# Channel attention and a gated convolution on one core: the first batch's rows dealt anew, weight conversion through PSUM, and the first softmax in another order

## The chip, the cores and the metric

One Trainium2 chip, of which the kernel uses one core. The metric is the device time of one execution in microseconds, as the median of several runs.

## The reference

Four batches of 6336 positions by 256 channels. An attention over channels is made of q and k, applied to v, and its result goes through a gated convolution over positions.

```python
qn = q / (np.linalg.norm(q, axis=1, keepdims=True) + 1e-06)
kn = k / (np.linalg.norm(k, axis=1, keepdims=True) + 1e-06)
s = kn.transpose(0, 2, 1) @ qn / tau          # 256 x 256 per batch, summed over 6336 positions
a = np.exp(s - s.max(-1, keepdims=True))
a /= a.sum(-1, keepdims=True) + 1e-09
x = v @ a                                      # 6336 x 256 per batch
# gated convolution, 5 taps over the positions, weights conv_w per channel
gate = sigmoid(sum_k conv_w[k] * x shifted by 4 - k positions)
out = (gate * (x @ w_val)) @ w_out
```

All data are fp32, but the three weights of the convolution stage, w_val, conv_w and w_out, arrive as 64-bit floats.

## The kernel before, in words

**Two streams of work.** The scores of a batch need all of its q and k before the softmax can be taken; the outputs of a batch need its softmax. So the kernel runs the scores of a later batch beside the outputs of an earlier one. Only the first batch has nothing beside it: its scores, its softmax and the first chunks of its outputs form a prologue of some 85 us.

**Scores by groups.** The 6336 positions of a batch are 49 rows of 128 positions (row j holds positions j, 49 + j and so on, one per partition) and a rest of 64. They are loaded in 17 groups: group 0 has one row and the rest, groups 1 to 16 three rows each. `score_group(b, g)` (L166) works on one group. The tile `raw` (six buffers) holds q and k of the group. A row can go to TensorE in two ways, chosen by `nw` (L171 to L174): the first `nw` rows of a group go unsplit, as fp32 matmuls of k by q; the other rows are split. For a split row ACT makes a rounded copy `hi` (L192), POOL the difference to it (L193), and TensorE does three products of the parts for each half of the channels (L226). One cast and one difference cover all split rows of a group. In a page of the profile, an unsplit row is four matmul records and a split row six.

**The norms.** ACT squares the group (L209, or L205 for the first row that a sum takes, which is written straight into it) into `sq`, two buffers. The squares are added to one of two sums: rows j < `nv` by VectorE to `acc_ps` in PSUM, the others by POOL to `acc` in SBUF (both L214). Before, batch 0 has `nw, nv = (3, 2)` for groups 0 to 10 and `(2, 3)` from group `SIDE` = 11 on. In batch 1 the first `LEAD` groups are unsplit; every other group is split whole, with `nv` = 2.

**The weights.** `load_weights(part)` (L105) loads the 64-bit words on SP's queue: part 0 is w_val, tau and conv_w, part 1 w_out. `prepare_weights(part)` (L124) is a generator that turns them into fp32 on VectorE in integer and float steps (L132 to L154), each step followed by a yield; its intermediate `f` lies in SBUF, in the tile that takes the result. For w_out a rounded part `wo_hi` (ACT, L149) and a rest `wo_lo` are made. The loads stand in the loop over the first batch's groups at n = 6, and from n = 9 on two steps of each part follow each group.

**The softmax.** `softmax(b)` (L236) is a generator, moved on one stage by each `tick()` (L466): sum the two norm sums and copy the scores out of PSUM (L240, L242); column sums with TensorE (L245, L247); square root, and for batch 0 a dummy exponential that loads ACT's table (L252, L254); reciprocals, scaling and the minimum on VectorE (L256 to L265); exponentials (L268); normalisation (L270 to L275); split into `w` (L278, L279); transposes of the result (L285); their copy (L289); product with w_val (L294); its split (L298, L299). With the first split done the gate's products can run, with the last the values'.

**Outputs by chunks.** v is handled in 13 chunks of 508 positions a batch. `transpose_v` (L326) turns a chunk and splits it into `v_hi` and `v_lo`; `conv` (L352) makes x for the taps (matmuls at L345 into `x_ps`) and applies the taps on ACT (L359) and VectorE (L361); `sigmoid`, `value` (`val_ps`, L374), `split_g` and `finish` (L404, L414) follow.

**What sets the order.** The calls in L476 to L563 are the program order. From it a planner builds the queue of each engine ahead of time, with its own estimate of when instructions become ready; earlier calls go first, and what is called under `tc.high_priority()` (every tick) goes ahead of other work. `behind(engines)` (L433) puts what is called in it, on each named engine, behind the last instruction that was marked in `marks` for that engine. On the chip each engine takes its queue in order. In the prologue, `run_group` (L453) issues the matmuls of a group, and `split_group` (L445) everything before them and the load of the group `PREFETCH` = 4 ahead. The prologue does `LEAD` groups of batch 1 between the stages of the first softmax. In the loop over the 52 chunks, `due` (L531) spreads the groups that are left evenly over the first 36 chunks.

## Time and profile before

| what | value |
|---|---|
| median of 3 runs | 657.26 us (657.15 to 657.44) |
| the profiled execution, its own time | 658.18 us |
| its span in the profile | 656.3 us |
| mean granted TensorE clock | 0.996 |
| busy: PE, VectorE, ACT, POOL | 97%, 80%, 71%, 55% |
| scores of batch 0, last matmul (L226) starts | 54.03 us |
| first matmul of the outputs (L345) | 70.69 us |

PE is TensorE, PEld its weight loads, DVE VectorE, ACT ScalarE, POOL GpSimd. A line of the timeline gives start and length in us, the engine, the line of the kernel, the operation, what it writes and reads, and in square brackets how long the engine had been idle before and what ended this. A line of the groups gives count, busy time in us and mean duration in ns. Matmuls are pipelined and their ends are modelled, so that a matmul's length is more than the distance to the next one, and the distance is what counts. The span begins with the first instruction; the execution's time has about 2 us around it.

### The profile page before, as it was taken

What the parts mean: (1) busy time and instruction counts of PE and PEld (TensorE: products, weight loads), DVE (VectorE), ACT (ScalarE), POOL (GpSimd) and SP (SyncE); (2) the same over time, 40 slices, a digit from 0 to 9 for tenths busy, and PEclk for the clock granted to TensorE, in tenths of its full rate; (3) what the DMA queues carried; (4) which work ended last, traced back from release to release, by engine and by line L of the source; (5) the groups of instructions that cost most, each with busy time, mean ns of one, the idle gap of its engine ahead of it and who ended that gap; (6) DMA issues with size and microseconds to landing.
All of it is one profiled execution on the core that took longest, in us unless ns stands there. A gap on an engine that the chain in (4) does not pass through costs nothing.

```text
span 656.3 us, 10656 instructions
## 1 busy us (share of the span) xinstructions
PE 637.8 (97%) x4008; PEld 571.1 (87%) x4008; DVE 523.0 (80%) x832; ACT 466.1 (71%) x607; POOL 360.8 (55%) x173
## 2 busy tenths in 40 slices
PE   7989999999999999999998999999999999999996
PEld 5868799989979999999997998998999798888886
DVE  3898689787878688778788688778778888888894
ACT  4565978867888768668698687767777756655564
POOL 2442796965837769659565497766763222312220
PEclk9999999999999999999999999999999999999999
DMA  8999874555635565545564365563222343443213
GB/s 268 322 328 337 267 225 152 161 166 165 179 103 176 188 195 176 173 132 170 175 184 121 109 217 158 189 185 104 65 78 71 118 126 95 121 129 104 65 50 100
DMA packets 107875, 105.75 MB, mean 161 GB/s; under 512 B 5744, under 2 KB 107312, under 8 KB 107824
## 3 DMA queue, kind: packets, MB, share of 16 engines
q1 hardware_dynamic: 81520, 79.24, 39.0%
q10 hardware_dynamic: 26304, 25.84, 13.9%
q8 instruction: 31, 0.51, 0.3%
q14 instruction: 20, 0.16, 0.1%
HBM read 79.11 MB, written 25.95 MB: 160 GB/s over the span
## 4 chain that ended last, share of the span: by engine, by line
PE 85%; ACT 5%; DVE 4%; POOL 2%; DMA 2%; issue 1%; SPq 1%; ACTq 0%; POOLq 0%
PE o_ps L404 20%; PE x_ps L345 20%; PE val_ps L345 19%; PE s_ps L226 18%; PE t_ps L335 6%; POOL hi L193 1%; ACT sq L209 1%; PE o_ps L294 1%; DMA raw<-in_k_dram 1%; DVE acc_ps L214 1%; ACT hi L192 1%; DVE gate L361 1%; DMA v_raw<-in_v_dram 1%; DVE gate L374 1%; ACT gate L367 0%
## 5 line engine op out<-in xcount | busy, mean ns | idle before, releaser
L361 DVE SCALAR_TENSOR_TENSOR gate<-x_ps,wa,gate 128x508 f32<-128x508 f32 (+1 forms) x416 | 275.4, 716 | 15.7 <-ACT gate L359 14.6
L193 POOL TENSOR_TENSOR hi<-raw,hi 128x1536 fp32r<-128x1536 f32 (+2 forms) x54 | 167.8, 3110 | 94.5 <-ACT hi L192 94.5
L388 POOL TENSOR_TENSOR g_lo<-gate,g_hi 128x1016 fp32r<-128x1016 f32 (+1 forms) x50 | 116.6, 2332 | 145.2 <-ACT g_hi L387 130.6
L214 DVE TENSOR_TENSOR acc_ps<-acc_ps,sq 128x512 f32<-128x512 f32 (+1 forms) x134 | 93.4, 697 | 74.8 <-ACT sq L209 71.6
L345 PE MATMUL x_ps<-v_hi,w 128*128 128x512 f32 (+1 forms) x416 | 139.1, 394 | 0.0
L345 PE MATMUL val_ps<-v_hi,w 128*128 128x508 f32 (+1 forms) x416 | 133.9, 383 | 0.8 <-ACT o_sb L414 0.7
L226 PE MATMUL s_ps<-hi 128*128 128x256 f32 (+1 forms) x852 | 121.1, 287 | 7.4 <-ACT hi L192 4.0
L226 PEld LDWEIGHTS s_ps<-hi 128*128 128x128 f32 (+1 forms) x852 | 110.7, 190 | 13.9 <-ACT hi L192 5.5
L404 PE MATMUL o_ps<-wo_hi,g_hi 128*128 128x256 f32 x400 | 113.2, 283 | 1.7 <-ACT g_hi L383 1.5
L414 ACT COPY o_sb<-o_ps 128x512 f32<-128x512 f32 x99 | 58.2, 589 | 79.1 <-PE o_ps L404 77.9
L404 PE MATMUL o_ps<-wo_lo,g_hi 128*128 128x256 f32 x400 | 112.1, 280 | 0.0
L404 PE MATMUL o_ps<-wo_hi,g_lo 128*128 128x256 f32 x400 | 111.7, 280 | 0.0
L209 ACT ACTIVATE sq<-raw 128x1536 f32<-128x1536 f32 (+3 forms) x69 | 96.0, 1393 | 16.5 <-DVE acc_ps L214 7.9
L214 POOL TENSOR_TENSOR acc<-acc,sq 128x512 f32<-128x512 f32 x58 | 76.4, 1318 | 39.7 <-ACT sq L209 39.3
L345 PEld LDWEIGHTS x_ps<-v_hi,w 128*128 128x128 f32 x416 | 78.2, 190 | 14.3 <-DVE gate L361 0.2
L345 PEld LDWEIGHTS val_ps<-v_hi,w 128*128 128x128 f32 x416 | 77.1, 188 | 14.5 <-ACT o_sb L414 0.9
L359 ACT ACTIVATE gate<-x_ps,wa 128x508 f32<-128x508 f32 (+1 forms) x104 | 68.2, 671 | 20.5 <-PE x_ps L345 20.2
L336 ACT CAST v_hi<-t_ps 128x512 fp32r<-128x512 f32 (+1 forms) x104 | 55.8, 569 | 36.2 <-PE t_ps L335 36.2
L345 PE MATMUL x_ps<-v_lo,w 128*128 128x512 f32 (+1 forms) x208 | 80.2, 386 | 0.0
L345 PE MATMUL val_ps<-v_lo,w 128*128 128x508 f32 (+1 forms) x208 | 79.2, 381 | 0.0
L374 DVE TENSOR_TENSOR gate<-val_ps,gate 128x508 f32<-128x508 f32 (+1 forms) x104 | 64.3, 657 | 18.3 <-ACT gate L367 14.0
L404 PEld LDWEIGHTS o_ps<-wo_hi,g_hi 128*128 128x128 f32 x400 | 75.2, 188 | 3.1 <-ACT g_hi L383 1.7
(84 smaller groups left out, 799.3 us busy)
## 6 DMA issues: line engine op xcount, KB each, us to landing
raw<-in_q_dram SPq DMA_DIRECT2D x64, 384.0 KB
raw<-in_k_dram SPq DMA_DIRECT2D x64, 384.0 KB
v_raw<-in_v_dram SPq DMA_DIRECT2D x44, 512.0 KB
out_dram<-o_sb ACTq DMA_DIRECT2D x48, 384.0 KB
out_dram<-o_sb ACTq DMA_DIRECT2D x48, 124.0 KB
v_raw<-in_v_dram SPq DMA_DIRECT2D x4, 384.0 KB
raw<-in_q_dram SPq DMA_DIRECT2D x4, 128.0 KB
raw<-in_k_dram SPq DMA_DIRECT2D x4, 128.0 KB
```

The source lines that it names most:

```text
L193: nc.gpsimd.tensor_tensor(hi[r, js, :, 1, :], raw[r, js, :, :], hi[r, js, :, 0, :].bitcast(F32), ALU.subtract)
L209: nc.scalar.activation(sq[0:np_, ja:jb], raw[0:np_, ja:jb], AF.Square)
L214: eng.tensor_tensor(st[key][0:np_], st[key][0:np_], sq[0:np_, j], ALU.add)
L226: nc.tensor.matmul(st["s"][:, h, :], lhs, rhs, start=False, stop=stop and h == NH - 1 and n_ == len(ops) - 1)
L336: nc.scalar.copy(th[:, h, 0:w], tp[:, 0:w])
L345: nc.tensor.matmul(ps, wt[:, which, ws, ch, hs], vs[:, ch, lo:hi_], start=n_ == 0, stop=n_ == 3 * NH - 1)
L359: nc.scalar.activation(gate[:, h, 0:w], x_ps[:, 0:w], AF.Copy, scale=cw[:, h, 0:1])
L361: nc.vector.scalar_tensor_tensor(gate[:, h, 0:w], x_ps[:, tap:tap + w], cw[:, h, tap:tap + 1], gate[:, h, 0:w], ALU.mult, ALU.add)
L374: nc.vector.tensor_tensor(gate[:, h, 0:w], val_ps[:, 0:w], gate[:, h, 0:w], ALU.mult)
L388: nc.gpsimd.tensor_tensor(gl[:, :, 0:w], gate[:, :, 0:w], gh[:, :, 0:w].bitcast(F32), ALU.subtract)
L404: nc.tensor.matmul(o_ps[:, u * C:(u + 1) * C], gs[:, h, off:off + P], ws[:, h, :], start=n_ == 0, stop=n_ == 3 * NH - 1)
L414: marks["ACT"] = nc.scalar.copy(o_sb[:, j:j + len(pair), :], o_ps[:, 0:len(pair) * C].rearrange("p (j c) -> p j c", c=C))
```

## The change

- Rows of batch 0: `nw, nv` are (3, 2) for group 0, (1, 3) for groups 1 to 5 (`EARLY` = 6), then (2, 2) for even and (3, 1) for odd groups.
- `LEAD` is 4 instead of 5: four groups of batch 1 in the prologue.
- The weights come in three parts, all loaded at n = 1, into buffers of other tiles ("gate", "o_sb") and one of their own. The intermediate of the conversion lies in PSUM. The parts are converted one after the other, three or four steps after each group from n = 7 on, on VectorE behind the last add of the norms. `wo_hi` is made by a copy on ACT behind the first softmax.
- The first softmax: the transposes of the first chunk come right behind the last scores of batch 0, the column sums behind these; the groups of batch 1 stand elsewhere between the ticks. More instructions are marked.

```diff
--- before.py
+++ after.py
@@ -17,10 +17,10 @@
 
 P = 128
 GROUP = 3
-LEAD = 5
+LEAD = 4
 PREFETCH = 4
 VLEAD = 2
-SIDE = 11
+EARLY = 6
 HALO = 4
 ROWS = 508
 
@@ -93,42 +93,47 @@
 
 
     WORDS = 2 if w_val.dtype == I64 else 1
-    NA = NH * C + NH * K
-    wa = const.tile([P, NA], F32, name="wa")
-    wb = const.tile([P, NH * C], F32, name="wb")
-    wv_sb = wa[:, 0:NH * C].rearrange("p (h e) -> p h e", h=NH)
-    cw = wa[:, NH * C:].rearrange("p (h k) -> p h k", h=NH)
+    NW = NH * C
+    wa = const.tile([P, NW + NH * K], F32, name="wa")
+    wb = const.tile([P, NW], F32, name="wb")
+    wv_sb = wa[:, 0:NW].rearrange("p (h e) -> p h e", h=NH)
+    cw = wa[:, NW:].rearrange("p (h k) -> p h k", h=NH)
     wo_hi = const.tile([P, NH, C], F32R, name="wo_hi")
     wo_lo = const.tile([P, NH, C], F32R, name="wo_lo")
+    parts_w = {"val": wa[:, 0:NW], "conv": wa[:, NW:], "out": wb}
     w_raw = {}
 
-    def load_weights(part):
-        src, w = ((w_val, wa), (w_out, wb))[part]
-        if WORDS == 2:
-            pool, tag = ((split_p, "hi"), (w_p, "o_sb"))[part]
-            raw = pool.tile([P, w.shape[1], WORDS], I32, name="w_raw", tag=tag)
-            src = src.bitcast(I32)
-        else:
-            raw = w.rearrange("p (n o) -> p n o", o=1)
-        w_raw[part] = raw
-        nc.sync.dma_start(out=raw[:, 0:NH * C, :].rearrange("p (h e) o -> p h (e o)", h=NH),
-                          in_=src.rearrange("(h p) e -> p h e", p=P))
-        if part == 0:
-            nc.sync.dma_start(out=tau_sb, in_=tau.broadcast_to([P, 1]))
-            src = conv_w.bitcast(I32) if WORDS == 2 else conv_w
-            for h in range(NH):
-                nc.sync.dma_start(
-                    out=raw[:, NH * C + h * K:NH * C + (h + 1) * K, :],
-                    in_=src[:, h * P * WORDS:(h + 1) * P * WORDS].rearrange("k (p o) -> p k o", o=WORDS))
+    def load_weights():
+        for part, w in parts_w.items():
+            if WORDS == 2:
+                tag = {"val": "gate", "out": "o_sb"}.get(part)
+                raw = (w_p if tag else const).tile([P, w.shape[1], WORDS], I32, name="w_raw", tag=tag or "c_raw")
+            else:
+                raw = w.rearrange("p (n o) -> p n o", o=1)
+            w_raw[part] = raw
+            if part == "conv":
+                src = conv_w.bitcast(I32) if WORDS == 2 else conv_w
+                nc.sync.dma_start(out=tau_sb, in_=tau.broadcast_to([P, 1]))
+                for h in range(NH):
+                    nc.sync.dma_start(out=raw[:, h * K:(h + 1) * K, :],
+                                      in_=src[:, h * P * WORDS:(h + 1) * P * WORDS].rearrange("k (p o) -> p k o", o=WORDS))
+            else:
+                src = {"val": w_val, "out": w_out}[part]
+                src = src.bitcast(I32) if WORDS == 2 else src
+                nc.sync.dma_start(out=raw.rearrange("p (h e) o -> p h (e o)", h=NH),
+                                  in_=src.rearrange("(h p) e -> p h e", p=P))
 
     def prepare_weights(part):
 
 
 
-        w = (wa, wb)[part]
+
+        w = parts_w[part]
+        n = w.shape[1]
         if WORDS == 2:
             lo, up = w_raw[part][:, :, 0], w_raw[part][:, :, 1]
-            f = w.bitcast(I32)
+            fs = ps.tile([P, 512], F32, name="w_ps", tag="bank")[:, 0:n]
+            f = fs.bitcast(I32)
             nc.vector.tensor_scalar(f, up, 0x1FF, 15, ALU.bitwise_and, ALU.logical_shift_left)
             yield
             nc.vector.scalar_tensor_tensor(lo, lo, 17, f, ALU.logical_shift_right, ALU.bitwise_or)
@@ -145,18 +150,15 @@
             yield
             nc.vector.tensor_tensor(up, up, f, ALU.bitwise_or)
             yield
-            if part:
-                nc.scalar.copy(wo_hi.rearrange("p h e -> p (h e)"), up.bitcast(F32))
-            dst = w if part == 0 else wo_lo.rearrange("p h e -> p (h e)")
-            nc.vector.scalar_tensor_tensor(dst, lo, 2.0 ** -35, w, ALU.mult, ALU.mult)
-            if part == 0:
+            dst = wo_lo.rearrange("p h e -> p (h e)") if part == "out" else fs
+            nc.vector.scalar_tensor_tensor(dst, lo, 2.0 ** -35, fs, ALU.mult, ALU.mult)
+            if part != "out":
                 yield
-                nc.vector.tensor_tensor(w, w, up.bitcast(F32), ALU.add)
-        elif part:
-            wof = wb.rearrange("p (h e) -> p h e", h=NH)
-            nc.scalar.copy(wo_hi, wof)
-            nc.vector.tensor_tensor(wo_lo, wof, wo_hi.bitcast(F32), ALU.subtract)
-        if part == 0:
+                nc.vector.tensor_tensor(w, fs, up.bitcast(F32), ALU.add)
+        elif part == "out":
+            nc.vector.tensor_copy(wo_hi, wb.rearrange("p (h e) -> p h e", h=NH))
+            nc.vector.tensor_tensor(wo_lo, wb.rearrange("p (h e) -> p h e", h=NH), wo_hi.bitcast(F32), ALU.subtract)
+        if part == "conv":
             yield
             tc.keep_in_program_order(nc.vector.reciprocal(rtau, tau_sb))
 
@@ -169,7 +171,7 @@
         n = groups[g][1]
         raw = raws.pop((b, g))
         if b == 0:
-            nw, nv = (GROUP, 2) if g < SIDE else (2, 3)
+            nw, nv = (GROUP, 2) if g == 0 else (1, 3) if g < EARLY else (2, 2) if g % 2 == 0 else (GROUP, 1)
         else:
             nw, nv = (GROUP, 1 if g else 2) if b == 1 and g < LEAD else (0, 2)
         parts = [(P, 0, n)]
@@ -211,7 +213,9 @@
             if j in where:
                 continue
             eng, key = (nc.vector, "acc") if j < nv else (nc.gpsimd, "side")
-            eng.tensor_tensor(st[key][0:np_], st[key][0:np_], sq[0:np_, j], ALU.add)
+            add = eng.tensor_tensor(st[key][0:np_], st[key][0:np_], sq[0:np_, j], ALU.add)
+            if key == "acc":
+                marks["DVE"] = add
 
         def mms(np_, j):
             r = slice(0, np_)
@@ -223,8 +227,8 @@
                 else:
                     ops = [(hi[r, j, 1, x, hs], hi[r, j, 0, y, :]) for x, y in ((0, 0), (0, 1), (1, 0))]
                 for n_, (lhs, rhs) in enumerate(ops):
-                    nc.tensor.matmul(st["s"][:, h, :], lhs, rhs, start=False,
-                                     stop=stop and h == NH - 1 and n_ == len(ops) - 1)
+                    marks["PE"] = nc.tensor.matmul(st["s"][:, h, :], lhs, rhs, start=False,
+                                                   stop=stop and h == NH - 1 and n_ == len(ops) - 1)
 
         def clear():
 
@@ -239,7 +243,7 @@
         acc = soft_p.tile([P, 2, C], F32, name="acc_all")
         nc.vector.tensor_tensor(acc, st["acc"], st["side"], ALU.add)
         s = soft_p.tile([P, NH, C], F32, name="s")
-        nc.scalar.copy(s, st["s"])
+        marks["ACT"] = nc.scalar.copy(s, st["s"])
         yield
         n_ps = ps.tile([P, 512], F32, name="o_ps", tag="bank")
         nc.tensor.matmul(n_ps[:, 0:C], ones, acc[:, 0, :], start=True, stop=True)
@@ -262,7 +266,7 @@
         for h in range(NH):
             nc.vector.scalar_tensor_tensor(s[:, h, :], s[:, h, :], nk[:, h:h + 1], r, ALU.mult, ALU.mult)
         m = soft_p.tile([P, NH], F32, name="m")
-        nc.vector.tensor_reduce(m, s, axis=AX.X, op=ALU.min)
+        marks["DVE"] = nc.vector.tensor_reduce(m, s, axis=AX.X, op=ALU.min)
         yield
         for h in range(NH):
             marks["ACT"] = nc.scalar.activation(s[:, h, :], s[:, h, :], AF.Exp, scale=-1.0, bias=m[:, h:h + 1], accum_out=z[:, h:h + 1])
@@ -332,7 +336,7 @@
         tp = ps.tile([P, 512], F32, name="t_ps", tag="bank")
         for j in range(-(-w // P)):
             np_ = min(P, w - j * P)
-            nc.tensor.transpose(tp[:, j * P:j * P + np_], src[0:np_, j, h * P:(h + 1) * P], ident[0:np_, 0:np_])
+            marks["PE"] = nc.tensor.transpose(tp[:, j * P:j * P + np_], src[0:np_, j, h * P:(h + 1) * P], ident[0:np_, 0:np_])
         nc.scalar.copy(th[:, h, 0:w], tp[:, 0:w])
         nc.vector.tensor_tensor(tl[:, h, 0:w], tp[:, 0:w], th[:, h, 0:w].bitcast(F32), ALU.subtract)
 
@@ -474,10 +478,9 @@
 
 
     for n in range(NG):
-        if n == 6:
-            load_weights(0)
-            load_weights(1)
-            prep.extend(prepare_weights(part) for part in range(2))
+        if n == 1:
+            load_weights()
+            prep.extend(prepare_weights(part) for part in parts_w)
         if n == NG - 4:
             load_upto(NG + 1)
             with tc.issue_after(last_load[0].ins):
@@ -487,36 +490,40 @@
                 for nv in range(1, VLEAD + 1):
                     load_v(*step(nv))
         run_group()
-        if n >= 9:
-            for gen in prep:
-                for _ in range(2):
-                    next(gen, 0)
+        if n > EARLY:
+            with behind("DVE"):
+                for _ in range(3 + n % 2):
+                    while prep and next(prep[0], 0) is not None:
+                        prep.pop(0)
     for gen in prep:
         for _ in gen:
             pass
-    prep.clear()
-    run_group()
     tick()
-    tick()
+    with tc.high_priority(), behind("PE", "ACT"):
+        for h in range(NH):
+            transpose_v(*step(0), h)
+    with behind("PE"):
+        tick()
+    with behind("ACT"):
+        run_group()
     tick()
     with behind("PE", "ACT"):
-        run_group()
-        for h in range(NH):
-            transpose_v(*step(0), h)
-    tick()
-    tick()
-    with behind("ACT"):
         run_group()
     tick()
     tick()
     tick()
+    tick()
     with behind("ACT"):
-        for n in range(3, LEAD):
+        for n in range(2, LEAD):
             run_group()
+    tick()
     for h in range(NH):
         conv(*step(0), h)
     while stages:
         tick()
+    if WORDS == 2:
+        with behind("ACT"):
+            nc.scalar.copy(wo_hi.rearrange("p h e -> p (h e)"), w_raw["out"][:, :, 1].bitcast(F32))
     for h in range(NH):
         transpose_v(*step(1), h)
     with behind("ACT"):
```

## The prediction

> **What bounds the kernel now.** I read the page first, for the engines' shares; then the windows of 25 us over the whole span, for the stretches where TensorE is not full; then the timeline of the first 90 us and of the one long gap behind it, and the duration of matmuls by stretch.
>
> ```profile
> span 656.3 us, 10656 instructions
> PE 637.8 (97%) x4008; PEld 571.1 (87%) x4008; DVE 523.0 (80%) x832; ACT 466.1 (71%) x607; POOL 360.8 (55%) x173
> 25.00:50.00 25.00, 22.20 (x111) 19.07 (x111) 24.27 (x35) 15.26 (x15) 12.01 (x9) 1.00 1.08 335
> 75.00:100.00 25.00, 23.69 (x150) 20.54 (x149) 21.53 (x34) 20.66 (x22) 23.31 (x11) 1.00 0.71 220
> 350.00:375.00 25.00, 22.31 (x144) 20.27 (x143) 17.67 (x30) 20.12 (x31) 9.64 (x5) 0.93 0.38 119
> ```
>
> The columns of a window are its length, then busy time (instructions) of PE, PEld, DVE, ACT and POOL, the granted clock, the DMA share and GB/s. TensorE is full in most windows, so the end comes earlier only by what is taken from TensorE's own work, its gaps, or its time at a low clock. In 25 to 50 us VectorE is full and TensorE is not: that is the stage that the change rebuilds.
>
> ```profile
> L226 PE MATMUL s_ps<-raw x6: 634/634/634, 9.7 to 11.9; 128*128 128x256 f32 x6
> L226 PE MATMUL s_ps<-raw x11: 379/379/379, 13.8 to 16.0; 128*128 128x256 f32 x11
> 4.31 20.04 PE L226 MATMUL s_ps<-raw 128*128 128x256 f32 x70 [1.91 <-DMA raw<-in_k_dram]
> 23.75 14.84 PE L226 MATMUL s_ps<-raw 128*128 128x256 f32 x68
> 92.69 2.15 PE s_ps L226 x18
> ```
>
> An unsplit row is 4 instructions. From 23.75 us on they start every 14.84/68 = 0.218 us, 0.87 us a row. A split row is 6 instructions at 2.15/18 = 0.119 us, 0.72 us a row. Until about 13 us the same unsplit instruction lasts 634 ns instead of 379, and six start within 2.2 us, one every 0.43 us: TensorE works at half rate there, although the granted clock reads 1.00. It has no gap from 4.31 to 38.6 us.
>
> ```profile
> 35.78 1.48 ACT L209 ACTIVATE sq<-raw 128x1536 f32<-128x1536 f32 x1 [3.43 <-DVE acc_ps L214]
> 40.15 0.86 PE L226 MATMUL s_ps<-hi 128*128 128x256 f32 x5 [1.44 <-POOL hi L193]
> 44.47 0.86 PE L226 MATMUL s_ps<-hi 128*128 128x256 f32 x5 [0.97 <-POOL hi L193]
> 54.03 1.06 PE L226 MATMUL s_ps<-hi 128*128 128x256 f32 x6
> 56.18 0.69 DVE L240 TENSOR_TENSOR acc_all<-acc_ps,acc 128x512 f32<-128x512 f32 x1
> 58.12 0.70 PE L245 MATMUL o_ps<-acc_all,ones 128*128 128x256 f32 x2
> 59.19 0.37 ACT L252 ACTIVATE o_ps<-o_ps 128x258 f32<-128x258 f32 x1 [1.69 <-PE o_ps L247]
> 69.12 0.62 ACT L278 CAST w<-a 128x512 fp32r<-128x512 f32 x1
> 70.69 0.47 PE L345 MATMUL x_ps<-v_hi,w 128*128 128x512 f32 x1
> ```
>
> VectorE, busy with the weight conversion, holds the squares (3.43 us), these hold the casts, and TensorE's first split rows wait for POOL. With the waits for the casts themselves TensorE loses some 3 us from 38.6 to 44.5 us. The scores of batch 0 end at 54.03 + 6 x 0.119 = 54.8 us; the sum of squares follows at 56.2 us, its column sums on TensorE only at 58.1 us, queued behind the first rows of batch 1; the weights of batch 0 reach TensorE at 70.7 us.
>
> **The change, part by part.** First the rows. Unsplit rows of batch 0 fall from 44 to 34, split rows rise from 6 to 16 (two in each of groups 1 to 5, one in each even group from 6): 10 x 0.15 = 1.5 us less for TensorE. But groups 1 to 5 now pass through ACT and POOL before TensorE can finish them, and the load of the weights moves ahead of group 5's.
>
> ```profile
> 8.03 0.63 ACT L205 ACTIVATE acc<-raw 128x512 f32<-128x512 f32 x1 [2.61 <-DMA raw<-in_k_dram]
> 11.33 1.48 ACT L209 ACTIVATE sq<-raw 128x1536 f32<-128x1536 f32 x1 [1.72 <-DMA raw<-in_k_dram]
> 20.34 1.48 ACT L209 ACTIVATE sq<-raw 128x1536 f32<-128x1536 f32 x1 [0.75 <-DVE acc_ps L214]
> 24.72 1.48 ACT L209 ACTIVATE sq<-raw 128x1536 f32<-128x1536 f32 x1 [2.90 <-DMA raw<-in_k_dram]
> 28.66 1.48 ACT L209 ACTIVATE sq<-raw 128x1536 f32<-128x1536 f32 x1 [2.46 <-DMA raw<-in_k_dram]
> 351.43 1.04 ACT L387 CAST g_hi<-gate 128x1016 fp32r<-128x1016 f32 x1 [0.26 <-DVE gate L374]
> L388 POOL TENSOR_TENSOR g_lo<-gate,g_hi 128x1016 fp32r<-128x1016 f32 (+1 forms) x50 | 116.6, 2332 | 145.2 <-ACT g_hi L387 130.6
> L193 POOL TENSOR_TENSOR hi<-raw,hi 128x512 fp32r<-128x512 f32 x6 | 7.9, 1313 | 6.2 <-ACT hi L192 6.2
> ```
>
> Groups 1, 2, 6, 7 and 8 land at 8.0, 11.3, 20.3, 24.7 and 28.7 us; from 2 to 6 that is 2.25 us a group. Today the weights sit around group 7 and hold it back by 24.7 - 22.6 = 2.1 us and group 8 by 28.7 - 27.0 = 1.7 us, 3.8 us together. The new order issues them right behind group 4, so group 5 lands at 18.1 + 3.8 = 21.9 us. A cast and a split of two rows have no row of their own; the nearest, 1016 wide, take 1.04 and 2.33 us (bounds: twice a 512 split, 2.6 us, and no less than 1.3). Both lie on TensorE's path when a group comes late.
>
> Group 1: its unsplit row ends at 9.7 us, cast 9.1, POOL 11.4; then 12 split instructions at half rate, 2.9 us, 14.3. Group 2: 1.7 us at half rate, 16.0; from here I take full rate, 1.4 us, 17.4. Groups 3 and 4 at 0.87 + 1.43: 19.7 and 22.0. Group 5: cast 23.0, POOL 25.3, TensorE 26.7, after a gap of 2.4 us. Groups 6 to 16: 27 unsplit rows, 23.5 us, and 6 split, 4.3 us: 54.5 us. POOL has two items of 1.28 to 1.31 in each of these groups, 2.6 us against TensorE's 2.53 on average, and starts 1.4 us ahead: it just keeps up. So TensorE's 3 us of waits and 1.5 us of work go, and 4.2 us of later starts in groups 1 to 5 eat them. Gain 0.3 us; bounds -2 (POOL at 2.6 us a pair, later groups waiting on it) and +2.8 (group 5 not held).
>
> VectorE's part:
>
> ```profile
> 24.77 0.45 DVE L136 TENSOR_SCALAR wa<-w_raw 128x522 int32<-128x522 int32 x1
> 30.36 1.76 DVE L146 TENSOR_TENSOR w_raw<-w_raw,wa 128x522 int32<-128x522 int32 x1
> 32.49 1.70 POOL L214 TENSOR_TENSOR acc<-acc,sq 128x512 f32<-128x512 f32 x1 [0.94 <-ACT sq L209]
> L214 DVE TENSOR_TENSOR acc_ps<-acc_ps,sq 128x512 f32<-128x512 f32 x37 | 25.8, 696 | 9.7 <-ACT sq L209 8.5
> ```
>
> Nineteen of the new 29 conversion steps are 512 wide. In SBUF they ran from 0.4 to 1.8 us, and POOL's adds beside them 1.7 instead of 1.3. With the intermediate in PSUM none has a row; the nearest is the add on PSUM, 0.70 us (bounds 0.4 and 1.8). At 0.70 they cost 13.3 us, about today's 15, in groups 7 to 9 and 12 to 14. There VectorE needs up to 3.5 us a group, but has one or two adds instead of two or three and catches up in 10, 11, 15 and 16: its last add ends near 53.7 us, beside POOL's 53.8, and acc_all near 54.5, not 56.9. The Trainium skill (VectorE: DVE Perf Modes, Why PSUM operands drop a tier) says that an operand in PSUM takes the doubled fp32 rate from single-source steps. By it the 0.45 us steps become 0.7 us, about 2 us more over both parts, and by the old rate the sum would be those 2 us smaller; both lie beside TensorE's work here.
>
> The softmax:
>
> ```profile
> 61.85 0.87 PE t_ps L335 x8
> 62.15 0.70 DVE L214 TENSOR_TENSOR acc_ps<-acc_ps,sq 128x512 f32<-128x512 f32 x1
> 63.80 1.28 DVE L337 TENSOR_TENSOR v_lo<-t_ps,v_hi 128x512 fp32r<-128x512 f32 x2
> 66.83 1.47 ACT L209 ACTIVATE sq<-raw 128x1536 f32<-128x1536 f32 x1
> ```
>
> Eight transposes now stand behind the last score, 0.87 us, to 55.4 us, then the column sums, 58.12 to 59.19 today, 1.0 us, to 56.4. (If chunk 0's values landed after 54.5 us, the column sums and the rows of batch 1 would wait behind the transposes; they are issued with the last loads of batch 0.) Then a clear (512 wide, 0.2 us) and four groups instead of five: 8 + 36 instructions at 0.217 us, 9.6 us, to 66.2, and the transposes of the weights, so the first x_ps at 66.5. The chain beside it took 69.74 - 59.19 = 10.5 us, of which an add of 0.7, two v_lo of 0.64 and 0.9 of the squares (66.83 to 68.30, while the reciprocals were done at 67.3) came from outside; these are queued elsewhere now. So the weights are there between 64.0 and 67.0. I take 66.7 for x_ps. Today's 70.7 contains the fifth group, 2.6 us, so the like is 68.1: gain 1.4 us with the 0.3 in it. The fifth group's three rows are split in the loop, 2.15 for 2.6 us: 0.45 us. The final copy to wo_hi moves behind the softmax, about 0.6 us on ACT (as the cast of w at 69.12) before its first reader, hidden by the transposes and values that come before; without that cover it costs 0.6. The 1.3 us of gaps from 75 to 100 us (25.00 less 23.69 in the second window above) I leave as they are.
>
> Sum: 1.85 us off the profiled execution, whose own time is 658.2 us, 1.9 around its span. The median stands 0.9 under it: 657.3 - 1.9 = 655.4 us.
>
> **The rivals.** First, faster because of a gap far behind the change: four groups ahead instead of five shift the later batches. The last group of batch 2 comes one step later, and as the first of a step's two groups, not the second.
>
> ```profile
> 354.89 0.28 PE L404 MATMUL o_ps<-wo_hi,g_lo 128*128 128x256 f32 x1
> 357.86 0.53 PE L226 MATMUL s_ps<-hi 128*128 128x256 f32 x1 [2.69 <-ACT hi L192]
> 356.00:358.00 2.00, 0.14 (x1) 0.14 (x2) 2.00 (x5) 2.00 (x3) 0.06 (x1) 0.99 0.31 103
> 358.00:360.00 2.00, 2.00 (x6) 1.61 (x7) 1.06 (x3) 1.99 (x3) 2.00 (x1) 0.50 0.53 122
> 360.00:362.00 2.00, 2.00 (x8) 1.58 (x7) 0.66 (x1) 1.98 (x2) 2.00 (x2) 0.66 0.10 35
> ```
>
> Here TensorE stands from 355.0 to 357.9 us, 2.9 us, and then runs 2 us at a clock of 0.50 and 2 at 0.66: 1.0 + 0.7 = 1.7 us. If the new order of the groups avoids it, 4.6 us more go: 650.8 us. For it: the other two batches, where the softmax starts with a step's first group, have no gap of this size. Against: ACT's exponentials and table load stand ahead of the casts in any order.
>
> Second, group 5 is not held by the weights (they land beside it, or are issued later): scores end near 52, and 655.4 - 2.5 = 652.9 us.
>
> Third, slower: the splits in groups 1 to 5 keep TensorE at half rate. It left the half rate at 13 us only after 8.6 us without a gap; now it waits from 9.7 to 11.4, and 2.4 us ahead of group 5. At half rate a group costs 1.7 + 2.9 = 4.6 us: group 1 at 14.3, then 18.9, 23.5, 28.1, 32.7 for group 5, against 26.7. That is 6 us lost: 661.4 us; half of it, if the rate rises in group 3, 658.4. It decides from the point where waits in the stretch from 9 to 16 us hold the rate down. Against: after the 2.9 us gap the clock was back within 4 us of dense work. The Trainium skill (TensorE: Matmul & The Clock Gate, HAM oscillation — how this bites in real kernels) warns against gaps over about 3.4 us, after which the array runs at half clock. By this 2.4 us would be safe; the 2.9 us gap above was punished all the same, so the measured row decides.
>
> Fourth, no change: the chain keeps its intrusions (weights at 67.0 or later) and the gaps from 75 to 100 us grow by one: 656.6 us.
>
> **How the numbers follow.** Forecast 0.35, own range 653.9 to 656.9; the gap goes 0.24 (650.8); group 5 free 0.12 (652.9); half rate 0.17 (658.4 to 661.4); no change 0.12. What can be told from no change is 0.2%, 1.3 us. Two thirds of the forecast's own range lies beyond it: faster 0.24 + 0.24 + 0.12 = 0.60; same 0.11 + 0.12 - 0.01 = 0.22; slower 0.18. The range runs from 650.6, the gap gone, to 659.2, the half rate until group 3 with some POOL lag.
>
> **What would show it.** Group 5's first square near 22 us and a TensorE gap of 2 to 3 us before its split rows; matmuls of 379 ns from 16 us on; no wait for POOL between 27 and 54 us; last score at 54.5; column sums near 55.5; first x_ps at 66.7. Wrong if TensorE waits for POOL after group 6, if the unsplit instruction still lasts 634 ns past 17 us, if x_ps waits for the weights' cast, or if TensorE's gap at a later softmax comes, goes or moves by more than 2 us.

## The result and the profile after

The changed kernel takes 660.12 us (median of 4 runs, 659.92 to 661.46) against 657.2 us before: 2.9 us more, where 655.4 us was forecast. The ratio of the runs is given as 1.0056, 95% interval 1.0037 to 1.0074 (the quotient of the two medians is 1.0044), so it is slower by about half a per cent. The profiled execution took 660.24 us, with a span of 658.5 us; the forecast for it was 658.2 - 1.85 = 656.35, so 3.9 us are to be found.

The page of the kernel after, busy time of the engines:

```profile
PE 637.0 (97%) x4034; PEld 571.3 (87%) x4034; DVE 522.3 (79%) x837; ACT 471.1 (72%) x613; POOL 382.8 (58%) x184
```

Its windows (length; busy time of PE, PEld, DVE, ACT, POOL; granted clock, DMA share, GB/s):

```profile
25.00:50.00 25.00, 25.00 (x127) 22.66 (x128) 22.94 (x45) 16.62 (x15) 21.92 (x18) 0.94 1.03 322
24.58:28.00 3.42, 3.09 (x13) 3.00 (x14) 3.14 (x5) 2.70 (x3) 1.86 (x3) 0.50 1.10 349
```

TensorE is busy for 0.8 us less than before, POOL for 22 us more. VectorE no longer fills the stretch from 25 to 50 us; POOL nearly does (21.92 of 25). In this execution a low clock stands at 24.58 us: 3.42 us at 0.50, beginning inside a gap of TensorE. It isn't what made the change slower: the other three executions have a mean granted clock of 0.999 to 1.000, which leaves no room for such a stretch (one alone brings the mean to 0.997), and they took 659.92, 659.99 and 661.46 us. The low clock that the profile before had at 358 to 362 us isn't there any more (from 340 to 395 us the clock is 1.00, in the windows below).

The timeline of the kernel after, from the first groups to the first products:

```profile
21.38 1.04 ACT L194 CAST hi<-raw 128x1024 fp32r<-128x1024 f32 x1 [3.35 <-DMA raw<-in_k_dram]
...
24.91 2.71 PE L230 MATMUL s_ps<-hi 128*128 128x256 f32 x11 [2.04 <-POOL hi L195]
...
30.90 0.69 DVE L143 TENSOR_SCALAR w_ps<-w_ps 128x512 int32<-128x512 int32 x1
...
54.38 1.06 PE L230 MATMUL s_ps<-hi 128*128 128x256 f32 x6
...
55.04 0.69 DVE L244 TENSOR_TENSOR acc_all<-acc_ps,acc 128x512 f32<-128x512 f32 x1 [1.10 <-POOL acc L216]
...
56.15 0.60 PE L249 MATMUL o_ps<-acc_all,ones 128*128 128x256 f32 x2
...
57.01 1.05 ACT L340 CAST v_hi<-t_ps 128x512 fp32r<-128x512 f32 x2
...
57.95 0.37 ACT L256 ACTIVATE o_ps<-o_ps 128x258 f32<-128x258 f32 x1
...
60.91 0.70 DVE L216 TENSOR_TENSOR acc_ps<-acc_ps,sq 128x512 f32<-128x512 f32 x1 [1.34 <-ACT sq L211]
...
61.52 1.76 DVE L262 RECIPROCAL o_ps<-o_ps 128x256 f32<-128x256 f32 x1
...
67.80 0.62 ACT L282 CAST w<-a 128x512 fp32r<-128x512 f32 x1
...
68.47 0.50 PE L349 MATMUL x_ps<-v_hi,w 128*128 128x512 f32 x1 [0.21 <-ACT w L282]
```

Group 5 lands at 21.4 us, and TensorE waits 2.04 us for its split. The last scores start at 54.38 us, 0.35 later than before. The column sums come 2.0 us earlier than before (56.15 against 58.12), but the long reciprocal, at 60.28 before, comes at 61.52: squares and casts of the first chunk now stand ahead of the square root, and an add that waits 1.34 us for its squares stands ahead of the reciprocal. The first products start 2.2 us earlier than before, with one group (2.6 us) less ahead of them. So at the door of the loop (the first products) nothing is won: in like terms it opens 0.4 us later. The rest of the 2.2 us that the span grew is lost behind it.

The loop of the kernel after, in windows around the softmaxes of batches 1 and 2:

```profile
185.00:235.00 50.00, 47.36 (x319) 42.80 (x319) 39.05 (x67) 41.96 (x62) 29.17 (x13) 1.00 0.51 151
340.00:395.00 55.00, 52.43 (x356) 47.67 (x355) 44.02 (x75) 44.95 (x64) 31.08 (x15) 1.00 0.53 156
```

TensorE's waits there from 185 to 235 us (what waited, for what, us in total, times, longest):

```profile
PE s_ps L230 <- POOL hi L195: 1.2, 2, 0.6
PE t_ps L339 <- ACT at L293: 0.9, 1, 0.9
PE val_ps L349 <- ACT o_sb L418: 0.6, 1, 0.6
```

The same two windows of the kernel before:

```profile
185.00:235.00 50.00, 49.21 (x340) 44.98 (x339) 39.25 (x69) 40.29 (x56) 32.88 (x15) 1.00 0.56 167
340.00:395.00 55.00, 52.31 (x349) 47.87 (x348) 42.34 (x75) 43.82 (x61) 31.64 (x15) 0.97 0.51 157
```

At batch 1 TensorE stands 50 - 47.36 = 2.64 us after, 0.79 before. At batch 2 it stands 2.57 us after and 2.69 before, but before this was one gap with a low clock behind it; after it is several short waits. So something new costs near 2 us at batch 1 and stands in the place of the gap at batch 2, though the loop over the chunks is not in the diff.

### The profile page after: what moved, and what is told of

Read it like the earlier page. It is cut to its first block, busy times and chain, and to the rows that moved or that the text cites. A ratio compares the mean times of both kernels' runs of the same rounds, so it can differ in the third digit from the quotient of the medians.

```text
span 658.5 us, 10744 instructions
## 1 busy us (share of the span) xinstructions
PE 637.0 (97%) x4034; PEld 571.3 (87%) x4034; DVE 522.3 (79%) x837; ACT 471.1 (72%) x613; POOL 382.8 (58%) x184
## 4 chain that ended last, share of the span: by engine, by line
PE 81%; ACT 9%; DMA 3%; issue 2%; POOL 2%; DVE 1%; SPq 1%; ACTq 0%; POOLq 0%
PE o_ps L408 20%; PE s_ps L230 19%; PE x_ps L349 18%; PE val_ps L349 17%; PE t_ps L339 6%; POOL hi L195 2%; DMA raw<-in_k_dram 2%; ACT hi L194 2%; ACT sq L211 1%; PE o_ps L298 1%; ACT gate L371 1%; DMA raw<-in_q_dram 1%; ACT L371 1%; DVE gate L365 1%; SPq L74 1%
## 5 line engine op out<-in xcount | busy, mean ns | idle before, releaser
L195 POOL TENSOR_TENSOR hi<-raw,hi 128x1536 fp32r<-128x1536 f32 (+3 forms) x60 | 183.1, 3057 | 106.6 <-ACT hi L194 106.6
L216 DVE TENSOR_TENSOR acc_ps<-acc_ps,sq 128x512 f32<-128x512 f32 (+1 forms) x129 | 90.0, 698 | 80.1 <-ACT sq L211 77.7
L230 PE MATMUL s_ps<-hi 128*128 128x256 f32 x930 | 135.2, 291 | 6.9 <-POOL hi L195 6.9
L230 PEld LDWEIGHTS s_ps<-hi 128*128 128x128 f32 x930 | 123.0, 193 | 13.1 <-POOL hi L195 8.7
L216 POOL TENSOR_TENSOR acc<-acc,sq 128x512 f32<-128x512 f32 x63 | 82.7, 1313 | 16.4 <-ACT sq L211 15.5
L194 ACT CAST hi<-raw 128x1536 fp32r<-128x1536 f32 (+3 forms) x60 | 77.6, 1299 | 10.7 <-DMA raw<-in_k_dram 10.7
```

Of the source, the lines that this page charges most:

```text
L194: cast = nc.scalar.copy(hi[r, js, :, 0, :], raw[r, js, :, :])
L195: nc.gpsimd.tensor_tensor(hi[r, js, :, 1, :], raw[r, js, :, :], hi[r, js, :, 0, :].bitcast(F32), ALU.subtract)
L216: add = eng.tensor_tensor(st[key][0:np_], st[key][0:np_], sq[0:np_, j], ALU.add)
L230: marks["PE"] = nc.tensor.matmul(st["s"][:, h, :], lhs, rhs, start=False, stop=stop and h == NH - 1 and n_ == len(ops) - 1)
```

## The experiments

Four theories for the loss went into them. **First**, the gap ahead of group 5, made by the weights' loads. **Second**, POOL: at 2.6 us a group it holds the sum of squares, and whatever comes earlier waits for it. **Third**, four groups of batch 1 ahead instead of five leave the loop too little slack. **Fourth**, formed when the third had fallen, a mark: the diff now marks the scores' copy in `softmax`, and `with behind("ACT"): split_group()` in the loop reads the marks.

**The weights after the groups.** The loads go back to n = 6. The first group of batch 1 is tied to TensorE too, which keeps TensorE's order as in the changed kernel.

```diff
-        if n == 1:
+        if n == 6:
             load_weights()
...
-    with behind("ACT"):
+    with behind("PE", "ACT"):
         run_group()
```

> The changed kernel with the weights' loads put back to where the kernel before has them (six groups on instead of one); the first group of batch 1 is also tied behind the column sums on TensorE, which is the order that the changed kernel has anyway. Theory 1 (the weights' loads ahead of group 5 are what costs: a gap of 2.0 us and then 3.4 us at half clock): group 5 lands near 18.1 us, no half clock in the first 55 us, the last score 3 to 4 us earlier than the 55.1 us of the changed kernel, and the time near 656.7 us. Theory 2 (POOL, with 2.6 us of work a group, sets the pace from group 6 on whatever comes before): last score within 1 us of 55.1, time near 660. Theory 3 (the loss comes from the loop, where four groups ahead leave one more group to be spread): scores earlier, but the time within 1 us of 660.1.

Measured: 662.8 us, 1.0085 [1.0065, 1.0105]. The wait that it shows, a line of the waits and of the timeline of this run:

```profile
PE o_ps L249 <- DVE acc_all L244: 2.3, 1, 2.3
```

```profile
54.92 0.69 DVE L244 TENSOR_TENSOR acc_all<-acc_ps,acc 128x512 f32<-128x512 f32 x1 [0.53 <-POOL acc L216]
```

And its windows:

```profile
36.00:55.00 19.00, 17.29 (x94) 15.20 (x92) 17.34 (x34) 12.49 (x13) 17.57 (x14) 1.00 1.05 324
57.27:64.09 6.82, 6.82 (x16) 4.55 (x16) 4.97 (x10) 4.28 (x10) 1.27 (x1) 0.50 1.10 348
```

The gap at 24 us is gone, and the last scores start 3.0 us earlier, at 51.42. But POOL, busy 17.57 of 19 us, ends the sum of squares when it did before: acc_all at 54.92 against 55.04. TensorE, in order, stands 2.3 us at the column sums and then runs 6.82 us at half clock. Of the six runs the one with a mean clock of 1.000 took 659.58 us, the others, at 0.992 to 0.996, 661.4 to 664.3. The first theory is right on the scores; the gain goes into a new wait, and what is lost beyond 660 us seems to go with the low clock.

**Group 5 unsplit.** No row of group 5 goes through ACT and POOL for TensorE.

```diff
-            nw, nv = ... (1, 3) if g < EARLY else ...
+            nw, nv = ... (1, 3) if g < EARLY - 1 else (GROUP, 2) if g < EARLY else ...
```

> The changed kernel with group 5 unsplit (three unsplit rows, two squares on VectorE), the weights' loads staying ahead of it; the same tie on TensorE. Theory 1 in its second half (the wait for cast and split of a late group opens the gap, and the gap brings the half clock): the gap of 2.0 us and the half clock go, TensorE does group 5 in 2.6 us from 21.4 us, group 6 starts near 24.0 us instead of 27.4, and the last score comes 2 to 3 us earlier: about 657.7 us. If the half clock is independent of that gap, it stays, and 1 us at most is won.

Measured: 662.08 us, 1.0082 [1.0057, 1.0108]. A line of the timeline of this run:

```profile
55.49 0.69 DVE L244 TENSOR_TENSOR acc_all<-acc_ps,acc 128x512 f32<-128x512 f32 x1 [0.52 <-POOL acc L216]
```

The same picture by another edit: last scores at 51.24 us, acc_all at 55.49, and TensorE waits 3.1 us for it, with half clock behind. The gap at group 5 is no loss by itself as long as POOL is late.

**Five groups ahead.** `LEAD = 5` in the changed kernel.

> The changed kernel with five groups of batch 1 ahead of the loop, as before the change. Theory 3 (the spread over the loop): the loop's share of the loss, about 1 us, comes back, and the prologue loses nothing in equal terms, as the waits of TensorE for the first softmax (0.9 us) are covered by the fifth group: 658 us. Theory 1: prologue as it is, 0.45 us more work for unsplit rows: 660 to 660.6 us. The gap and half clock at 24 to 28 us stay in either case.

Measured: 659.7 us, 1.0051 [1.0033, 1.0068]: the same as with four.

**Four groups ahead, alone.** `LEAD = 4` in the kernel before.

> The kernel before with four groups of batch 1 ahead of the loop instead of five, nothing else. Theory 3: slower by 1 us or more, 658.3 us, from later softmaxes falling on other chunks. Rival: the first softmax there takes 14.6 us against 12 us of filling work, so that TensorE stands some 2 us before the first x_ps, 659 us, while the 4.6 us gap and half clock at the softmax of batch 2 go or move.

Measured: 656.17 us, 0.9987 [0.9977, 0.9997], about 1 us faster than before; both theories expected it slower. Its windows at the two softmaxes:

```profile
185.00:235.00 50.00, 49.20 (x336) 44.94 (x335) 39.33 (x71) 44.12 (x63) 28.81 (x14) 1.00 0.53 161
340.00:395.00 55.00, 54.21 (x365) 49.30 (x364) 42.91 (x76) 48.62 (x67) 32.99 (x15) 1.00 0.53 160
```

The third theory falls. The gap of batch 2 and the low clock behind it are gone, as the first rival of the prediction had it: 0.79 us idle, the clock at 1.00. The gain may be the absent low clock alone: all 11 runs have a mean clock of 0.998 to 1.000, which leaves no room for one, and of the kernel before the eight of 25 runs that have 0.999 show much the same median, 655.9 us. What the changed kernel has in these places isn't due to `LEAD`.

**The loop without the mark.** The scores' copy is marked in the first softmax only.

```diff
-        marks["ACT"] = nc.scalar.copy(s, st["s"])
+        copied = nc.scalar.copy(s, st["s"])
+        marks["ACT"] = copied if b == 0 else marks["ACT"]
```

> The changed kernel with one mark less: the copy of the scores out of PSUM is marked for ACT in batch 0 alone, so that in the loop the casts and squares of the next group are no longer tied behind it. Up to the softmax of batch 1, TensorE's, ACT's and VectorE's queues stay as they are. Theory A (in the loop this mark is an added wait: at the softmaxes of batches 1 and 2 the next group's casts queue behind a copy that waits for the last scores): the prologue stays the same, from chunk 9 on the time of each chunk is 2 to 5 us earlier than in the changed kernel, 656 to 658 us. Rival (the loop's loss comes from four groups ahead and from where the last groups fall): the loop stays within 1 us, 659.5 to 660.5 us.

Measured: 655.9 us (654.9 to 658.2, 12 runs), 0.9987 [0.9973, 1.0001]; no run of it reaches the lowest of the changed kernel, 659.92. Its windows:

```profile
185.00:235.00 50.00, 49.16 (x336) 44.94 (x336) 39.34 (x71) 43.29 (x63) 29.25 (x14) 1.00 0.52 157
340.00:395.00 55.00, 54.22 (x368) 49.46 (x367) 44.27 (x77) 47.45 (x66) 32.93 (x15) 1.00 0.54 167
```

The idle time falls from 2.64 and 2.57 us to 0.84 and 0.78, 3.6 us together; the median falls by 4.2.

Its prologue has the queues of the changed kernel, but this execution has no low clock at group 5:

```profile
52.78 1.06 PE L230 MATMUL s_ps<-hi 128*128 128x256 f32 x6
...
55.84 0.69 DVE L244 TENSOR_TENSOR acc_all<-acc_ps,acc 128x512 f32<-128x512 f32 x1 [1.09 <-POOL acc L216]
...
56.58 0.70 PE L249 MATMUL o_ps<-acc_all,ones 128*128 128x256 f32 x2 [1.86 <-DVE acc_all L244]
```

The last scores start 1.6 us earlier than in the profile of the changed kernel, and the column sums come no earlier (56.58 against 56.15): TensorE stands 1.86 us for the sum of squares that POOL holds. So in this prologue POOL sets the column sums, and the low clock at group 5 does not.

**The mark alone.** The mark, for b > 0, added to the kernel before with `LEAD = 4`.

```diff
-        nc.scalar.copy(s, st["s"])
+        copied = nc.scalar.copy(s, st["s"])
+        marks["ACT"] = copied if b else marks.get("ACT")
```

> The kernel before with four groups ahead (656.2 us by itself) and one thing more: from batch 1 on the copy of the scores is marked for ACT, so that the next group's casts and squares queue behind it. Theory A (this added wait costs the loop some 4 us): 660 to 661 us, with the prologue unchanged up to chunk 8 and TensorE's waits at the softmaxes of batches 1 and 2 as in the changed kernel. Rival (the mark costs only together with the new prologue): within 1 us of 656.2 us.

Measured: 660.37 us, 1.0059 [1.0038, 1.008], 4.2 us above the same kernel without it. The timeline of the kernel without the mark, at the softmax of batch 1:

```profile
185.19 0.59 PE L245 MATMUL o_ps<-acc_all,ones 128*128 128x256 f32 x2
...
185.87 0.62 ACT L192 CAST hi<-raw 128x512 fp32r<-128x512 f32 x1
...
186.57 2.54 POOL L193 TENSOR_TENSOR hi<-raw,hi 128x512 fp32r<-128x512 f32 x2 [2.53 <-ACT hi L192]
...
188.09 1.28 ACT L252 ACT_TABLE_LOAD   x1
```

And with it:

```profile
184.03 0.59 PE L245 MATMUL o_ps<-acc_all,ones 128*128 128x256 f32 x2
...
185.31 1.28 ACT L252 ACT_TABLE_LOAD   x1 [0.50 <-DVE gate L361]
...
186.89 0.59 ACT L242 COPY s<-s_ps 128x512 f32<-128x512 f32 x1
...
187.37 1.14 ACT L192 CAST hi<-raw 128x512 fp32r<-128x512 f32 x2
...
188.07 2.53 POOL L193 TENSOR_TENSOR hi<-raw,hi 128x512 fp32r<-128x512 f32 x2 [5.19 <-ACT hi L192]
...
194.55 2.30 PE L226 MATMUL s_ps<-hi 128*128 128x256 f32 x17 [0.54 <-POOL hi L193]
```

Counted from the column sums (185.19 and 184.03), POOL gets its first cast after 1.4 us without the mark and after 4.0 us with it. The planner had put the casts of the next group first and the table load, square root and copy behind them. With the copy marked, the group has to stand behind the copy, and so behind the table load and the square root too. POOL has stood 5.19 us when it starts, and TensorE runs into it at 194.55. The fourth theory holds, in both directions and on two kernels. What is shown is the price of the mark; the chain over POOL is seen for a part of it. Of the 2.64 us at batch 1 of the changed kernel two waits for POOL make 1.2; 0.9 are a wait for ACT's copy of the transposed softmax (L293), which the kernels without the mark don't have there and no run takes apart.

**The deal alone.** The new `nw, nv` in the kernel before, nothing else.

```diff
-            nw, nv = (GROUP, 2) if g < SIDE else (2, 3)
+            nw, nv = (GROUP, 2) if g == 0 else (1, 3) if g < 6 else (2, 2) if g % 2 == 0 else (GROUP, 1)
```

> The kernel before with the new deal of the first batch's rows alone. Theory (TensorE saves 1.5 us, but POOL at 2.6 us a group holds the sums of squares, and VectorE's conversions stay as they are): last score 2 to 4 us earlier than 54.8, since group 5 is not held by the weights; acc_all no earlier than 55; time within 1.3 us of 657.3. Rival (the deal is what makes the change slow): slower by 2 us or more, 659.3 us.

Measured: 661.3 us (659.83 to 667.11), 1.0071 [1.0047, 1.0095]. Its windows:

```profile
36.00:39.16 3.16, 0.32 (x2) 0.32 (x3) 3.06 (x4) 1.78 (x2) 3.12 (x3) 1.00 1.07 356
39.16:42.58 3.42, 3.42 (x12) 2.88 (x11) 3.39 (x3) 0.62 (x1) 3.34 (x3) 0.50 1.10 349
```

Without the conversion in PSUM and spread out, VectorE is full (3.06 of 3.16 us) and POOL too. TensorE stands 4.0 us for POOL in the scores of batch 0, 2.9 of them in one wait that ends at 38.84, and has a low clock behind it; the last scores start at 55.38 us, acc_all at 58.52. So the rows alone are a loss of 4 us, as the rival had it. What they are worth beside the other parts no run shows.

**Late weights without the mark.** The loads at n = 6 and no mark in the loop; without the tie, the planner puts the column sums behind matmuls of batch 1 (26 in the trace, where 13 were expected).

> The kernel of the run before this one with the weights' loads put back to the sixth group, and without the tie of the run with late loads: the planner puts the column sums behind 13 matmuls of batch 1, which fill TensorE's wait for the sums of squares. Theory (scores 3 us earlier, but the sums of squares not, since POOL has 2.6 us a group): last score near 52.2, acc_all near 55, no wait of 2.3 us and no half clock at 57 us; first x_ps near 67.5; with the loop's gain 654.5 to 656.5 us. Rival (the half clock comes anyway, because the eight transposes and column sums keep TensorE's array little used): half clock near 57 us, 658 to 660 us.

Measured: 658.99 us, 1.0027 [1.0017, 1.0038]. The wait that decides:

```profile
PE o_ps L289 <- ACT a L279: 3.7, 1, 3.7
```

The last scores start at 51.80 us, acc_all comes at 55.10, column sums only at 59.88; TensorE runs out of rows and waits 3.7 us for the softmax. The 2.5 us again don't arrive.

**A lighter POOL.** To this, three edits: odd groups give POOL one sum of squares instead of two, the reciprocals go ahead of the adds of batch 1's groups, and w_out is converted in the first step of the loop.

```diff
-            nw, nv = ... else (2, 2) if g % 2 == 0 else (GROUP, 1)
+            nw, nv = ... else (2, 2) if g % 2 == 0 else (GROUP, 2)
...
     tick()
-    with behind("PE", "ACT"):
+    tick()
+    with behind("PE", "ACT", "DVE"):
         run_group()
     tick()
     tick()
-    tick()
...
         split_g(*now)
+        if n == 0:
+            for _ in prepare_weights("out"):
+                pass
+            nc.scalar.copy(wo_hi ...)
```

> The run before this one with three more edits: in odd groups from 7 on VectorE adds two squares and POOL one; w_out is converted beside chunk 0's outputs instead of before the softmax; the reciprocals stand ahead of the second group of batch 1 in program order. Theory (sums of squares and the queue on VectorE hold the first softmax): acc_all within 1 us of the last score, near 53; weights of batch 0 near 62 us; first x_ps near 64.5; 651 to 654 us. Rival (TensorE's filling work and ACT's order hold it): x_ps no earlier than 66.5, 655 us or more.

Measured: 653.89 us (653.58 to 654.58), 0.9951 [0.9934, 0.9968]: faster than both kernels. Its timeline:

```profile
50.90 0.69 DVE L244 TENSOR_TENSOR acc_all<-acc_ps,acc 128x512 f32<-128x512 f32 x1
...
51.03 1.06 PE L230 MATMUL s_ps<-hi 128*128 128x256 f32 x6
...
52.80 0.60 PE L249 MATMUL o_ps<-acc_all,ones 128*128 128x256 f32 x2
...
62.55 0.62 ACT L282 CAST w<-a 128x512 fp32r<-128x512 f32 x1
...
64.16 0.49 PE L349 MATMUL x_ps<-v_hi,w 128*128 128x512 f32 x1
```

Now the sum of squares is there before the last scores, the weights before TensorE asks for them, and the first products start at 64.16 us instead of 68.47. Up to its last matmul the profiled execution has no low clock. Some 1.5 us are given back at the first chunks: TensorE is idle for 38 - 34.44 = 3.6 us from 72 to 110 us, against 2.1 in the changed kernel. The three edits were not run apart, so their shares are open.

**The same with the weights early.** Loads at n = 1 again, all else as in the lighter kernel.

> The run with the lighter POOL with the weights' loads back at the first group, ahead of group 5, as the changed kernel has them; TensorE's queue stays the same. Theory 1 (the gap ahead of group 5, 2.0 us, and the half clock behind it): last score 2.5 to 3.5 us later, near 55, and with POOL no longer in the way all of it reaches the end: 656 to 657.5 us. Rival (the sums of squares hold the end anyway): within 1 us of 653.9 us.

Measured: 658.54 us, 1.002 [1.0006, 1.0035], 4.6 us more, 1 us beyond the range expected. A line of its timeline, then the window behind it:

```profile
26.05 2.52 PE L230 MATMUL s_ps<-hi 128*128 128x256 f32 x11 [2.05 <-POOL hi L195]
```

```profile
26.30:29.71 3.41, 3.41 (x15) 3.14 (x15) 3.10 (x6) 2.52 (x3) 1.85 (x2) 0.50 1.11 349
```

With POOL out of the way the first theory has its price: the 2.05 us gap and 3.41 us at half clock are back, and the first products start at 68.87 us instead of 64.16. The profiled execution, the slowest of twelve, has a second low stretch from 97.98 us, so part of the 4.6 us may lie there.

**The lighter kernel with five groups ahead.** `LEAD = 5`.

> The run with the lighter POOL with five groups of batch 1 ahead instead of four. If TensorE's filling work is what holds the first x_ps there (no wait of TensorE between 52 and 64 us), the fifth group moves x_ps 2.6 us on and costs 0.45 us for its unsplit rows; the loop of five groups has the gap and half clock at the softmax of batch 2 (4.6 us in the kernel before): 655 to 658 us. If the prologue had a hidden wait that a fifth group covers: 652 us.

Measured: 657.52 us, 1.0017 [1.0002, 1.0032], 3.6 us more than with four. Its low clock stands from 357.0 to 360.5 us, where the kernel before has one.

**The lighter kernel, warmed.** Six matmuls of zeros on TensorE ahead of the first group.

```diff
+    wp = ps.tile([P, 512], F32, name="warm_ps", tag="bank")
+    for _ in range(6):
+        nc.tensor.matmul(wp, zeros[:, 0:P], zeros, start=True, stop=True)
     for n in range(NG):
```

> The run with the lighter POOL with six matmuls of zeros on TensorE from 1.6 us on, while it waits for the first load; nothing else in its queue changes. Theory (TensorE runs at half rate up to 13 to 16.5 us, since it is not used densely enough in the first windows): full rate from 8 to 10 us on, last score 0.5 to 2 us earlier, 652 to 653.5 us. Rival (the loads set the pace of groups 1 to 5 anyway): full rate earlier, but the time within 0.5 us of 653.9.

Measured: 653.77 us (652.54 to 655.16), 0.9956 [0.9939, 0.9974]. Matmuls of its unsplit rows, with durations in ns (least, median, most) and first and last start:

```profile
L230 PE MATMUL s_ps<-raw x4: 379/379/454, 7.9 to 8.7; 128*128 128x256 f32 x4
```

Unsplit rows run at full rate (379 ns) by 7.9 us; the lighter kernel without these matmuls still had them at 628 to 634 ns between 13.9 and 15.2 us:

```profile
L230 PE MATMUL s_ps<-raw x4: 628/634/634, 13.9 to 15.2; 128*128 128x256 f32 x4
```
The last scores start 1.1 us earlier, and the span of the profiled execution is 1.0 us shorter (650.8 against 651.8). The medians can't be told apart, because half of the eight runs have a mean clock of 0.995 to 0.997; the four at 1.000 took 652.5 to 653.3 us, the four of the lighter kernel at 0.999 to 1.000 took 653.6 to 654.0.

## Why the prediction was wrong, and where it was right

**The step that failed** is in the part that costs the change: it priced the first softmax and the rows, and carried the loop over unchanged. "More instructions are marked" was never priced, although the loop reads the same marks. That mark costs 4.2 us, taken away (660.1 to 655.9) and added alone (656.2 to 660.4); the sign of the result hangs on it, since without it the change is at the time before (0.9987 [0.9973, 1.0001]). In the difference to the forecast it doesn't show as such, because the gap of batch 2, which the forecast kept, went at the same time (next paragraph). The question of what is queued behind an instruction that waits, asked of each new mark, would have led there: behind the marked copy stand the next group's casts, behind these POOL, behind POOL TensorE. Among the signs that would make it wrong the prediction named a gap at a later softmax that comes or goes, and both happened, but it had no mechanism for a new one.

**655.9 isn't a proof of 655.4.** In the forecast the gap of batch 2 stays. It went, with four groups ahead: idle and low clock there were 2.69 + 1.7 us before, 0.78 us without the mark. That was the first rival's gain (4.6 us by its count; four groups ahead alone brought 1.1), and in the changed kernel the mark's waits took its place, 2.57 us. Against it the prologue gave less than forecast. Two errors nearly cancel in 655.9; that it lies near the forecast is luck. It is also luck that 660.1 lies in the 658.4 to 661.4 us of the third rival, whose half rate was not there. (The first rival's 650.8 is 655.4 - 4.6; the 650.6 at the end of the range follows from no sum.)

**In the prologue**, point by point. Group 5's landing (21.9 forecast, 21.4 measured), the gap behind it (2.4; 2.04), and the PSUM step (0.70; 0.69) were right; so was full rate before 16 us, so that the third rival's half rate through five groups fell. POOL kept up with TensorE's rows, which wait for it nowhere from 26 to 55 us, but not with the sum of squares. In the profiled execution the last scores end at 55.1 us (54.38 + 6 x 0.119) and not at 54.5: the 2.04 us gap brought 3.42 us at half clock, a cost that the sum left out, although the prediction's own rows had the like behind the gap of batch 2. It decided nothing here. acc_all comes at 55.04 (54.5), held 1.10 us by POOL, and the column sums at 56.15 (55.5); where the low clock was absent, in the run without the mark, they came at 55.84 and 56.58.

**The softmax chain** was mis-sized most. The forecast let the squares, v_lo and the add go from the path. They changed their places instead: casts of the first chunk (1.05 us) ahead of the square root, and an add ahead of the reciprocal, for which VectorE stands 1.34 us. From the column sums to the weights' cast it is 67.80 - 56.15 = 11.7 us; before it was 69.12 - 58.12 = 11.0. The weights are there at 68.4 us (67.80 + 0.62), outside the 64.0 to 67.0 forecast, and TensorE waits for them. So the first products start at 68.47, not 66.7: 1.8 us of the 3.9. From 72 to 110 us TensorE is idle for 38 - 35.88 = 2.12 us, which the forecast left at 1.3: 0.8 more. The other 1.3 us lie in the loop. There the waits of the mark are about as long as the gap and the low clock that the forecast had kept, so against the forecast the mark's price and the gap's going hide each other, and I found no row for these last 1.3 us: their cause stays open.

**The second rival** (group 5 free) had its condition right: last scores near 52 in both runs that freed it. Its gain needed a sum of squares that is early too. With POOL late it was 662 to 663 us, or 659.0 without the mark; with POOL lighter and no mark, 653.9 against 658.5.

## What to carry to other kernels

A hint on order that later code reads again is an edit of that code: follow each place that reads it, and see what stands behind the instruction it now names. A stage gains only when all of its inputs come earlier: scores 3 us sooner were worth nothing until the sum of squares, on another engine, was sooner as well. And the parts of a change can have opposite signs: the new deal alone cost 4 us, the mark alone 4.2, four groups ahead alone won 1. So run the parts apart before they are judged.

## What the runs showed of the hardware

**The low clock goes by the use of a stretch, not by the length of one gap.** The trace keeps the times at which the granted clock changed. Within each of the 14 traces they lie a multiple of 3.413 us apart. In the lighter kernel with early weights the drops at 26.30 and 97.98 us are 71.68 us apart, 21 times 3.413; with the deal alone those at 39.16 and 360.02 us are 320.86 us apart, 94 times. So an execution has a grid of stretches of 3.413 us, and it lies differently in each: counted from the start of the span, the first edge is at 0.69 us in the changed kernel and at 2.81 in the lighter one.

One pair of gaps, 1.55 and 0.69 us, stands in two kernels at the same chunk, in the lighter kernel at 90.5 and 92.7 us and with early weights at 95.2 and 97.4. In the first an edge of the grid, at 91.55, cuts the longer one, and both stretches stay at full clock:

```profile
88.14:91.55 3.41, 2.32 (x20) 2.12 (x18) 3.41 (x7) 0.59 (x1) 3.33 (x3) 1.00 0.76 236
91.55:94.97 3.42, 2.26 (x11) 1.79 (x12) 3.42 (x6) 1.65 (x3) 0.95 (x1) 1.00 0.30 83
```

In the second all but 0.1 us of both lies in one stretch, and the low clock follows:

```profile
94.57:97.98 3.41, 1.26 (x10) 0.82 (x8) 3.41 (x7) 0.56 (x1) 2.56 (x2) 1.00 0.42 144
97.98:101.39 3.41, 3.32 (x8) 2.68 (x9) 3.41 (x6) 1.97 (x4) 0.00 (x0) 0.50 0.50 159
```

Neither gap is as long as 2 us, while the warmed kernel has one of 2.05 us at 9.4 us with the clock at 1.00 behind it. Over all traces, from the first record of the clock to 640 us, there are 13 drops. In the stretch ahead of each, TensorE was busy for 0.15 to 0.52 of the time (with the modelled ends of its matmuls), and of all other stretches at full clock only two were busy for so little (0.48 and 0.51). The low clock lasted one stretch in nine cases and two in four; what decides between them is not shown. A grid that lies differently each time fits a low clock that comes in some executions of a kernel and not in others.

The Trainium skill (TensorE: Matmul & The Clock Gate, HAM oscillation — how this bites in real kernels) puts the harmful gap at over about 3.4 us. The lengths at half clock here agree with that as the size of the gate's window; the gaps don't, at 2.04 and 2.05 us, nor does the pair of 1.55 and 0.69.

**The start.** TensorE works at half rate there, and the 1.00 of the windows says nothing about it: the records of the clock begin only at 14.34 us in the changed kernel, 16.46 in the lighter one and 6.23 with six matmuls of zeros ahead, and the windows show 1.00 where there is no record. The same instruction lasts 628 to 634 ns before that time and 379 ns after it.

**Runs of one kernel** differ by 3 us and more (654.9 to 658.2 us without the mark). The profiled one of these, the slowest at 658.2, has a low clock from 57.5 to 64.3 us and a mean clock of 0.991; six of the other eleven have 0.998 to 1.000, which leaves no room for such a stretch.
